# A bf16 three-part spread of 1/den, selectors built ahead of q, two ones columns in kv, and a later slot for one batch's numerators

The chip is one Trainium2, of which one core is used. The metric is the device time of one execution in microseconds (us); a run is repeated and the median quoted. TensorE is called PE here, VectorE DVE, ScalarE ACT and GpSimd POOL, as in the profile.

## The reference

Linear attention with phi(x) = elu(x) + 1 over 8 batches of 8 heads, 576 positions and 64 channels, then a two-layer feed-forward on 4608 tokens:

```python
q_p, k_p = phi(q), phi(k)                       # phi(x) = where(x > 0, x, exp(x) - 1) + 1
kv  = einsum('bhsd,bhse->bhde', k_p, v)
z   = k_p.sum(axis=2)
num = einsum('bhsd,bhde->bhse', q_p, kv)
den = einsum('bhsd,bhd->bhs', q_p, z) + 1e-6
x   = (num / den) -> [4608 tokens, 512]
h   = x @ w_in        # 512 -> 2048
g   = h - tanh(h)
out = g @ w_out       # 2048 -> 512
```

## The kernel before

The tokens go through the feed-forward in nine chunks (c = 0 to 8) of 512. While PE works on chunk c, the attention of batch c + 1 is threaded between its matmuls: lists s1 and s2 name what is emitted after the n-th group of four layer-one matmuls and after the n-th group of four layer-two matmuls (a slot). All loads are issued by POOL and cast to bf16 on the way. The parts that matter here (cuts marked `# ...`):

```python
def a_kv_cols(b, banks):                  # kv and z of batches 2 to 7
    ps = [banks()[:, 0:272].rearrange("p (i e) -> p i e", i=2) for hg in range(2)]
    for i in range(2):
        for j in range(J):                # J = 9
            for hg in range(2):           # the two halves of PE's rows, side by side
                r = slice(64 * hg, 64 * hg + 64)
                nc.tensor.matmul(ps[hg][:, i, :], kp[r, i, j]..., vp[r, i, j, :], ...)
    for hg in range(2):                   # vp: 128 columns of v and 8 columns of ones
        nc.vector.tensor_mul(kz_t[b][:, hg, :, 0:136], ps[hg], mask[:, hg, :, 0:136])

def b0_spread(pairs, n0):                 # batch 0: 1/den to 128 partitions, fp32 matmuls
    for n, p in enumerate(pairs):
        for t in range(4):
            nc.tensor.matmul(ps_all[:, 4 + t, 128 * (n0 + n):...], sel[r, p]..., rden_t[0][r, 0:128], ...)

# the opening, in order of emission
load_q(0); load_k(0); make_identity(nc, ident); load_v(0)
for f0, n in ((0, 256), (256, 256), (512, 512), (1024, 512), (1536, 512)):
    load_wi(f0, n)
load_k(1); load_wo(0); load_wo(1); load_q(1)
for i in (1, 0):
    nc.gpsimd.memset(v_b[i][:, 2], 1.0)
# ...
load_v(1); load_wo(2); load_wo(3)
# ... kv, den and num of batch 0
b0_spread((0, 2), 0)
b0_scale(0, ns0, 0, 0, 4); b0_scale(0, ns0, 0, 4, 8); b0_scale(2, ns0, 1)
b0_num(1, ns0)
# open2(): b0_spread((1, 3), 2); b0_scale(1, ...); b0_scale(3, ...)

# chunk c, batch n1 = c + 1
for p in range(NP + 1):                   # five numerator groups
    s2[(11 if c == 1 else 9) + p].append(lambda p=p: a_num(n1, p))
```

The first layer-one matmuls of chunk 0 are ordered by hand: two groups on pair 0 (halves of 256 columns), then open2, then the rest.

## Time and profile before

| | before |
|---|---|
| median (3 runs) | 294.0 us (293.95 to 294.2) |
| profiled span | 291.8 us at full PE clock |
| PE busy / DVE / ACT | 97% / 60% / 48% |
| transfers, 4 to 50 us | 197 to 209 GB/s without a pause |
| one 128x512 matmul, start to start | 216 ns |

In a profile line such as those in the prediction, the columns are: start (us from the span's start), length, engine, source line, operation, output<-inputs, shapes, count, and in brackets how long the engine sat idle before it and what released it. Lines of the chain of work that ended last have start, length and what it was. A busy PE is modelled, so pace is judged from matmul starts.

### The profile page before, as it was taken

Reading aid. Unit: us, or ns where it says so; the run is one execution under the profiler, and the core shown is the slowest. Engines: PE = TensorE matmul, PEld = TensorE weight load, DVE = VectorE, ACT = ScalarE, POOL = GpSimd, SP = SyncE. Lnnn points to the kernel's source line nnn. Section 1 sums busy time; section 2 is a strip of 40 time slices with the busy share of each in tenths; the row PEclk is TensorE's granted clock in tenths of the full one; section 3 lists DMA queues with packets and bytes.
Section 4 is the critical chain, followed back from the end, with each engine's and each line's share of the span. In section 5 each row is a group of like instructions: output and inputs, shape, how many; then the busy total and the mean of one; then the engine's idle time right before and its main releaser. Section 6 shows DMA issues by size and latency. Waiting matters only on the chain.

```text
span 291.8 us, 4476 instructions
## 1 busy us (share of the span) xinstructions
PE 284.2 (97%) x1775; PEld 134.5 (46%) x1803; DVE 174.8 (60%) x266; ACT 139.7 (48%) x168; POOL 33.1 (11%) x55
## 2 busy tenths in 40 slices
PE   8999999999999999999999999999999999999994
PEld 3544464454454444544444445444444444444443
DVE  4759958987458674776478637865581457106600
ACT  4838638846254733465345534751551155126411
POOL 8673030110030003000300030000000000000000
PEclk9999999999999999999999999999999999999999
DMA  6999999998989668955795579766117310130032
GB/s 96 198 204 212 208 207 213 214 168 145 253 158 159 170 131 135 200 139 127 134 223 131 120 137 196 144 142 139 32 34 168 73 36 0 42 84 20 0 74 72
DMA packets 39077, 38.94 MB, mean 133 GB/s; under 512 B 16336, under 2 KB 33808, under 8 KB 38288
## 3 DMA queue, kind: packets, MB, share of 16 engines
q0 software_dynamic: 17552, 18.35, 39.0%
q1 hardware_dynamic: 21344, 20.17, 30.5%
q8 instruction: 14, 0.23, 0.3%
q10 hardware_dynamic: 160, 0.13, 0.1%
q14 instruction: 7, 0.06, 0.1%
HBM read 43.91 MB, written 9.55 MB: 183 GB/s over the span
## 4 chain that ended last, share of the span: by engine, by line
PE 75%; DMA 18%; POOL 2%; issue 1%; SPq 1%; DVE 1%; ACT 1%; DVEq 0%; POOLq 0%
PE ps_all L366 37%; PE ps_all L387 32%; DMA w_out_sb<-in_moe_w_out_dram 6%; DMA w_in_sb<-in_moe_w_in_dram 3%; DMA rdb<-ds 3%; DMA out_dram<-osb 2%; PE ps_all L199 2%; DMA kraw<-in_k_dram 2%; PE ps_all L317 2%; DMA ds<-rden 1%; PE ps_all L276 1%; POOL v L419 1%; ACT osb L396 1%; SPq L401 0%; POOL qraw L90 0%
## 5 line engine op out<-in xcount | busy, mean ns | idle before, releaser
L366 PE MATMUL ps_all<-xT,w_in_sb 128*128 128x512 bf16 x558 | 126.5, 380 | 0.9 <-issue 0.2
L387 PE MATMUL ps_all<-w_out_sb,gT 128*128 128x512 bf16 x548 | 126.2, 380 | 0.7
L373 DVE TENSOR_TENSOR gT<-ps_all,th 128x1024 bf16<-128x1024 f32 x64 | 77.9, 1218 | 59.7 <-ACT th L372 59.7
L372 ACT ACTIVATE th<-ps_all 128x1024 f32<-128x1024 f32 x64 | 65.5, 1023 | 57.0 <-PE ps_all L366 46.4
L366 PEld LDWEIGHTS <-w_in_sb 128*128 128x128 bf16 x574 | 55.0, 98 | 66.0
L387 PEld LDWEIGHTS <-gT 128*128 128x128 bf16 x560 | 54.1, 98 | 64.7 <-issue 0.6
L396 ACT COPY osb<-ps_all 128x512 f32<-128x512 f32 (+1 forms) x36 | 20.8, 582 | 72.3 <-PE ps_all L387 55.9
L328 DVE TENSOR_TENSOR xT<-ps_all,rdb 128x512 bf16<-128x512 f32 x24 | 16.3, 689 | 13.7 <-PE ps_all L317 11.2
L134 ACT ACTIVATE e<-qraw 128x1152 bf16<-128x1152 bf16 x16 | 18.5, 1161 | 7.3 <-DMA qraw<-in_q_dram 7.3
L134 ACT ACTIVATE e<-kraw 128x1152 bf16<-128x1152 bf16 x15 | 17.4, 1162 | 0.1
L136 DVE TENSOR_TENSOR qp<-e,r 128x1152 bf16<-128x1152 bf16 x16 | 12.1, 758 | 7.8 <-ACT e L134 7.0
L136 DVE TENSOR_TENSOR kp<-e,r 128x1152 bf16<-128x1152 bf16 x15 | 11.4, 758 | 7.9 <-ACT e L134 7.0
L383 POOL COPY g<-qT 1x1 bf16<-1x1 bf16 x5 | 0.9, 182 | 119.7 <-DMA qT<-qp 119.7
L378 DVE TENSOR_TENSOR gT<-ps_all,th 128x512 bf16<-128x512 f32 x16 | 10.3, 686 | 2.3 <-ACT th L377 1.7
L377 ACT ACTIVATE th<-ps_all 128x512 f32<-128x512 f32 x16 | 9.2, 598 | 4.4 <-PE ps_all L366 3.2
L444 PE MATMUL ps_all<-zero 128*128 128x512 bf16 x29 | 9.3, 487 | 1.2 <-DVE zero L405 1.2
L317 PE MATMUL ps_all<-qT,kz 128*128 128x512 bf16 x28 | 10.1, 380 | 0.1
L135 DVE TENSOR_SCALAR r<-qraw 128x1152 bf16<-128x1152 bf16 x16 | 7.3, 453 | 1.9 <-DMA qraw<-in_q_dram 1.9
L199 PEld LDWEIGHTS <-kp 64*128 64x128 bf16 x216 | 6.4, 94 | 2.5 <-issue 2.5
L285 DVE RECIPROCAL rden<-den 128x144 f32<-128x144 f32 x7 | 7.4, 1052 | 0.2
L199 PE MATMUL ps_all<-vp,kp 64*128 64x136 bf16 x216 | 7.4, 220 | 0.0
L394 DVE COPY osb<-ps_all 128x128 f32<-128x128 f32 x1 | 0.3, 291 | 11.6 <-DMA out_dram<-osb 11.6
(84 smaller groups left out, 123.0 us busy)
## 6 DMA issues: line engine op xcount, KB each, us to landing
out_dram<-osb SPq DMA_DIRECT2D x70, 128.0 KB
rdb<-ds SPq DMA_DIRECT2D x12, 576.0 KB
kraw<-in_k_dram POOLq DMA_DIRECT2D x7, 576.0 KB, 7.1
qraw<-in_q_dram POOLq DMA_DIRECT2D x7, 576.0 KB, 9.2
v<-in_v_dram POOLq DMA_DIRECT2D x7, 576.0 KB, 11.9
w_out_sb<-in_moe_w_out_dram POOLq DMA_DIRECT2D x4, 512.0 KB, 16.0
w_in_sb<-in_moe_w_in_dram POOLq DMA_DIRECT2D x6, 256.0 KB, 8.6
qraw<-in_q_dram POOLq DMA_DIRECT2D x2, 288.0 KB, 4.4
```

The source lines that it names most:

```text
L134: return (lambda: nc.scalar.activation(e, x, AF.Exp), lambda: nc.vector.tensor_scalar(r, x, 0.0, 1.0, ALU.max, ALU.add), lambda: nc.vector ...
L136: lambda: nc.vector.tensor_tensor(y, e, r, ALU.min))
L199: nc.tensor.matmul(ps[hg][:, i, :], kp[r, i, j].rearrange("p h d -> p (h d)"), vp[r, i, j, :], start=(j == 0), stop=(j == J - 1))
L317: nc.tensor.matmul(ps, kz[:, p // 2, p % 2, 0:128], qT[:, p % 2, 0:8, p // 2, :], start=True, stop=True)
L328: nc.vector.tensor_mul(xT[:, p, S * b:S * b + 512].rearrange("p (j t c) -> p j t c", j=8, t=4), ps.rearrange("p j (t c) -> p j t c", t=4), ...
L366: nc.tensor.matmul(h, w_in_sb[:, 2 * (p % 2) + p // 2, fi * 128:(fi + 1) * 128], xT[:, p, c * 512:(c + 1) * 512], start=(n == 0), stop=(n ...
L372: nc.scalar.activation(th, h, AF.Tanh)
L373: nc.vector.tensor_sub(gT[:, fi:fi + 2, :], h, th)
L378: nc.vector.tensor_sub(gT[:, fi, :], h, th)
L387: nc.tensor.matmul(o, gT[:, fi, i * 128:(i + 1) * 128], w_out_sb[:, fi, :], start=(fi == 0), stop=(fi == NF - 1))
L396: nc.scalar.copy(osb[:, f0:f1], o[:, f0:f1])
L444: nc.tensor.matmul(ps_all[:, 0, :], zero[:, 0:128], zero, start=True, stop=True)
```

## The change

Its intent: make the second 1/den spread of batch 0 cheap (bf16 matmuls with 1/den split into three bf16 parts, where the trace has two records for each fp32 one), have the selectors ready long before, stream fewer columns in kv, and keep batch 2's numerators from meeting their late broadcast.

```diff
-    vp = const.tile([128, 2, J, 136], BF16, name="vp")
+    vp = const.tile([128, 2, J, 130], BF16, name="vp")
 ...
-        ps = [banks()[:, 0:272].rearrange("p (i e) -> p i e", i=2) for hg in range(2)]
+        ps = [banks()[:, 0:260].rearrange("p (i e) -> p i e", i=2) for hg in range(2)]
 ...
-            nc.vector.tensor_mul(kz_t[b][:, hg, :, 0:136], ps[hg], mask[:, hg, :, 0:136])
+            nc.vector.tensor_mul(kz_t[b][:, hg, :, 0:128], ps[hg][:, :, 0:128], mask[:, hg, :, 0:128])
+            nc.vector.tensor_mul(kz_t[b][:, hg, :, 128:136], ps[hg][:, :, 128:129].to_broadcast([128, 2, 8]),
+                                 mask[:, hg, :, 128:136])
 ...
+    def b0_split():                       # two halves, each a cast and a scalar_tensor_tensor
+        f = rden_t[0][:, 0:128]
+        nc.vector.tensor_copy(t1, f)
+        nc.vector.scalar_tensor_tensor(u, t1, part[:, 0:1], f, ALU.mult, ALU.add)
+        yield
+        nc.vector.tensor_copy(t2, u)
+        nc.vector.scalar_tensor_tensor(w, t2, part[:, 1:2], u, ALU.mult, ALU.add)
+        rden_t[0] = w
+        yield
+    def b0_spread3(pairs, n0):            # as b0_spread, with the bf16 selector sel3 and w
 ...
     load_q(0)
+    make_identity(nc, ident)
     load_k(0)
-    make_identity(nc, ident)
 ...
+    prepare()                             # selectors: moved here, ahead of phi(q), from s2[0] of chunk 0
 ...
     b0_kz(1)
+    next(split0)
     b0_spread((0, 2), 0)
 ...
     b0_scale(2, ns0, 1)
+    next(split0)
     b0_num(1, ns0)
     def open2():
-        b0_spread((1, 3), 2)
+        b0_spread3((1, 3), 2)
 ...
-                s2[(11 if c == 1 else 9) + p].append(lambda p=p: a_num(n1, p))
+                s2[min(12 + p, 15) if c == 1 else 9 + p].append(lambda p=p: a_num(n1, p))
 ...
-            order = [((0, 0), (0, 1)), ((2, 0), (2, 1), (0, 2), (0, 3), (2, 2), (2, 3)),
+            order = [((0, 0), (0, 1)), ((0, 2), (0, 3), (2, 0)), ((2, 1), (2, 2), (2, 3)),
                      [(p, fi) for p in (1, 3) for fi in range(4)]]
-                if n == 1:
+                if n == 2:
                     open2()
```

More of the change, by code (lines that the diff above doesn't have):

```diff
@@ L233, in b0_num @@
         nc.scalar.copy(ns[:, i::2, 0:8, :].rearrange("p a j t -> p a (j t)"), ps_all[:, b0:b0 + 2, :])
+    def b0_split():
+        f = rden_t[0][:, 0:128]
+        t1, t2, w = (rpool.tile([128, J * 16], BF16, name=n)[:, 0:128] for n in ("t1", "t2", "w"))
+        u = rpool.tile([128, J * 16], F32, name="u")[:, 0:128]
+        nc.vector.tensor_copy(t1, f)
[6 more added lines that the diff above has]
+    def b0_spread3(pairs, n0):
+        for n, p in enumerate(pairs):
+            for t in range(4):
+                r = slice(32 * t, 32 * t + 32)
+                nc.tensor.matmul(ps_all[:, 4 + t, 128 * (n0 + n):128 * (n0 + n) + 128],
+                                 sel3[r, p].rearrange("p h e -> p (h e)"), rden_t[0][r], start=True, stop=True)
     def b0_spread(pairs, n0):
@@ L419 @@
         nc.gpsimd.memset(v_b[i][:, 2], 1.0)
-    nc.gpsimd.memset(vp[:, :, :, 128:136], 1.0)
+    nc.gpsimd.memset(vp[:, :, :, 128:130], 1.0)
     load_v(1)
@@ L439, with prepare @@
         rest -= e0
+    def prepare():
+        for t in range(4):
+            nc.vector.tensor_copy(s8[32 * t:32 * t + 32].rearrange("q n h p -> q (n h p)"),
+                                  ident[32 * t:32 * t + 32, 32 * t:32 * t + 24])
+        s24 = rpool.tile([128, 2 * NP], F32, name="s24")
+        f8 = s8.rearrange("q n h p -> q n (h p)")
+        nc.vector.tensor_add(s24, f8[:, 1], f8[:, 2])
+        nc.vector.tensor_reduce(part[:, 0:1], s24, mybir.AxisListType.X, ALU.add, negate=True)
+        nc.vector.tensor_reduce(part[:, 1:2], f8[:, 2], mybir.AxisListType.X, ALU.add, negate=True)
+        nc.vector.tensor_add(s24, s24, f8[:, 0])
+        nc.vector.tensor_copy(
+            sel3, s24.rearrange("q (h p) -> q p h", h=2).unsqueeze(3).to_broadcast([128, NP, 2, 64]))
     def spin(n):
@@ L457 @@
     a_qT_pe(0, 1, side, "AA")
-    for t in range(4):
-        nc.scalar.copy(s8[32 * t:32 * t + 32, 0].rearrange("q h p -> q (h p)"),
-                       ident[32 * t:32 * t + 32, 32 * t:32 * t + 8])
     nc.scalar.copy(sel, s8[:, 0].rearrange("q h p -> q p h").unsqueeze(3).to_broadcast([128, NP, 2, 64]))
@@ L477 @@
     b0_kz(1)
+    split0 = b0_split()
+    next(split0)
     b0_spread((0, 2), 0)
@@ L482 @@
     b0_scale(2, ns0, 1)
+    next(split0)
     b0_num(1, ns0)
     def open2():
-        b0_spread((1, 3), 2)
+        b0_spread3((1, 3), 2)
         b0_scale(1, ns0, 2)
         b0_scale(3, ns0, 3)
-    def prepare():
-        for t in range(4):
-            nc.vector.tensor_copy(s8[32 * t:32 * t + 32, 1:3].rearrange("q n h p -> q (n h p)"),
-                                  ident[32 * t:32 * t + 32, 32 * t + 8:32 * t + 24])
-        s24 = rpool.tile([128, 2 * NP], F32, name="s24")
-        f8 = s8.rearrange("q n h p -> q n (h p)")
-        nc.vector.tensor_add(s24, f8[:, 1], f8[:, 2])
-        nc.vector.tensor_reduce(part[:, 0:1], s24, mybir.AxisListType.X, ALU.add, negate=True)
-        nc.vector.tensor_reduce(part[:, 1:2], f8[:, 2], mybir.AxisListType.X, ALU.add, negate=True)
-        nc.vector.tensor_add(s24, s24, f8[:, 0])
-        nc.vector.tensor_copy(
-            sel3, s24.rearrange("q (h p) -> q p h", h=2).unsqueeze(3).to_broadcast([128, NP, 2, 64]))
     for c in range(NC):
@@ L526 @@
             s2[4].append(lambda: (a_qphi(1, 1), load_q(2), load_k(2), load_v(2)))
-            s2[0].append(prepare)
             s2[7].append(lambda: (a_qT_pe(1, 0, side), a_kv(1, side), a_qT_pe(1, 1, side)))
```

## The prediction

> **What bounds the kernel now.** I read the page's busy table, then the chain of work that ended last, then the timeline of the stretches where TensorE (PE) has a gap. PE is the bound: it is busy 97% of 291.8 us, and the granted clock is 1.00 throughout. Busy is not peak, so I checked the pace: between 233 and 274 us the chain shows runs such as 38 layer-one matmuls in 8.37 us, 220 ns each, hardly above the 216 ns of four in 0.86 us elsewhere. Only work taken off PE, or a gap closed on PE, moves the end.
>
> ```profile
> PE 284.2 (97%) x1775; PEld 134.5 (46%) x1803; DVE 174.8 (60%) x266; ACT 139.7 (48%) x168; POOL 33.1 (11%) x55
> L366 PE MATMUL ps_all<-xT,w_in_sb 128*128 128x512 bf16 x558 | 126.5, 380 | 0.9 <-issue 0.2
> L199 PE MATMUL ps_all<-vp,kp 64*128 64x136 bf16 x216 | 7.4, 220 | 0.0
> ```
>
> The chain, however, does not run back through PE to the start. Asked for the first 60 us alone it reads (start, length, what):
>
> ```profile
> 2.78 6.18 DMA kraw<-in_k_dram
> 9.24 8.93 DMA w_in_sb<-in_moe_w_in_dram
> ...
> 22.39 0.66 POOL v L93
> 23.05 17.84 DMA w_out_sb<-in_moe_w_out_dram
> 40.89 0.04 issue
> 40.93 0.38 PE ps_all L387
> ```
>
> So the third quarter of w_out lands at 40.89 us and the first layer-two matmul that needs it starts 0.04 us later. Everything PE does before 40.9 us is off the path that sets the end, unless it becomes later than that landing. The busy table by stretches says why the landing is where it is: the columns are stretch, total, PE, PEld, DVE, ACT, POOL, clock, DMA share, GB/s.
>
> ```profile
> 4.00:24.00 20.00, 18.95 (x202) 9.88 (x202) 12.65 (x25) 12.94 (x21) 15.26 (x25) 1.00 1.24 197
> 24.00:41.00 17.00, 16.89 (x120) 8.88 (x120) 14.47 (x32) 11.17 (x17) 2.78 (x4) 1.00 1.23 209
> ```
>
> The transfers run at about 200 GB/s without a pause, and w_out's third quarter waits 17.84 us behind others already queued. It is limited by transfer rate, not by when it is issued. And PE already waits for it:
>
> ```profile
> 40.20 0.68 PE L164 MATMUL ps_all<-ident,qp 128*128 128x128 bf16 x9
> 40.93 1.02 PE L387 MATMUL ps_all<-w_out_sb,gT 128*128 128x512 bf16 x3
> ```
>
> The nine transposes' weight loads take 0.51 us from 40.19, so the next matmul could go at about 40.72; it goes at 40.93. PE is some 0.2 us early already.
>
> The opening, which most of the change concerns, is a ladder of short waits (the timeline, PE and DVE):
>
> ```profile
> 14.72 0.42 DVE L225 TENSOR_TENSOR kz<-ps_all,mask 128x256 bf16<-128x256 f32 x1
> 15.64 1.35 DVE L244 TENSOR_TENSOR xT<-ns,ps_all 128x256 bf16<-128x256 f32 x3 [0.50 <-PE ps_all L240]
> 16.09 1.01 ACT L233 COPY ns<-ps_all 128x1024 f32<-128x1024 f32 x1 [0.97 <-DVE xT L244]
> 16.12 0.71 PE L577 MATMUL ps_all<-xT,w_in_sb 128*128 128x256 bf16 x4
> 17.05 0.73 PE L240 MATMUL ps_all<-rden,sel 32*128 32x128 f32 x16 [0.22 <-DVE xT L244]
> ```
>
> The second spread of 1/den (17.05) starts only when DVE's third scaling ends (15.64 + 1.35 = 16.99).
>
> Batch 2's numerators meet a late DMA in the second chunk:
>
> ```profile
> 77.20 0.38 PE L317 MATMUL ps_all<-qT,kz 128*128 128x512 bf16 x1
> 77.41 1.03 PE L387 MATMUL ps_all<-w_out_sb,gT 128*128 128x512 bf16 x4
> 77.80 1.89 DVE L328 TENSOR_TENSOR xT<-ps_all,rdb 128x512 bf16<-128x512 f32 x3 [2.49 <-DMA rdb<-ds]
> 78.54 0.38 PE L317 MATMUL ps_all<-qT,kz 128*128 128x512 bf16 x1
> ```
>
> DVE waits 2.49 us for the broadcast 1/den, and the third numerator waits for its bank: its matmul could go at 77.41 + 4 x 0.216 = 78.27 and goes at 78.54, a gap of 0.27 us on PE.
>
> **What the skill says.** The Trainium skill, "PSUM — Partial Sum Buffer", section "PSUM bank collisions raise a hardware error", wants accesses guarded by bank. The trace agrees: the second spread writes other columns of the four banks that the third scaling reads, and starts 0.06 us after it. "FP8 and Floating Point Precision", "TensorE Precision Notes", gives true fp32 four passes. The trace agrees in direction: eight fp32 spread matmuls take 0.73 us (16 records), eight bf16 ones of batch 1, a little wider, 0.30 us. "TensorE: Matmul & The Clock Gate", section "Wait — 56ns, not 53.3ns?", spaces warm matmuls by columns / 2.4 GHz plus 2.5 ns: 216 ns for 512, as measured. "SBUF — State Buffer", "Who interferes with whom", says that DVE's two-port modes lock GpSimd out while it writes descriptors; no row of this trace shows such a lock by itself.
>
> **The change part by part.**
>
> *Selectors earlier.* The preparation takes 34.06 to 35.81, 1.75 us of DVE, in a stretch where PE streams without a gap: removing it there is worth nothing on PE. Its new place is after the masks (DVE is free at 3.50) and before the first q (5.42): 3.50 + 1.75 = 5.25, so it fits. Even 0.7 us late is harmless, as the next step waits for ACT until 6.6. Four ACT casts (0.81 us) go, but ACT's copy at 14.11 then waits for PE anyway (its matmuls end at 14.07): zero. The identity moved ahead of k delays k's issue by 0.6 us (2.78 to 3.4), but q occupies the transfers until about 6.7, so k's landing should not move.
>
> *Split and spread.* Batch 1's row of split operations took 0.24 + 0.37 us per half (44.78 to 45.43); for 128 columns about 0.22 + 0.35. The first half runs after kz: 15.16 to 15.78, so the first scaling goes from 15.64 to about 15.8 (0.15 later). The third scaling then ends near 17.15, and the second half ends near 17.75: the new spread can go at about 17.85, where the old one went at 17.05. It frees PE at 18.1 (0.23 us until the next matmul in batch 1, 46.16 to 46.39) against 17.93. But three more layer-one matmuls stand before it. The first two of those write banks 2 and 3, which ACT reads until 16.09 + 1.01 = 17.10; so they go at 17.2, and all three end at 17.85. Then three more until 18.75, a wait for the scaled pair (spread ends about 18.15, scaling of 0.68 until 18.9), then eight: 18.95 + 8 x 0.216 = 20.68. Before: 17.93 + 14 x 0.216 = 20.95. Gain 0.27 us, all of it before 40.9 us. It should turn into a longer wait for w_out: 0.2 + 0.27 = about 0.5 us. Value at the end: zero.
>
> *130 columns for 136.* The 36 matmuls of a batch run as 18 pairs on two halves of the rows, 1.17 us a batch in the chain, so 65 ns a pair with the switch of mode, close to the columns' 59 ns by the formula above. Six columns fewer save 6 / 2.4 = 2.5 ns a pair: 18 x 2.5 = 45 ns, six batches 0.27 us, an estimate. DVE pays: two operations become four. The main one stays near 0.42 (256 columns took 424 ns, 272 took 430), and the new one of 16 elements costs about 0.17 (a 128x32 copy took 184 ns), so some 0.3 us more a batch. kz was ready at 60.47 in the second chunk and used at 61.06; at 60.8 it still is in time, and later chunks have a slot more.
>
> *Num of batch 2 a slot later.* It closes the 0.27 us gap, as the broadcast is there by 77.8. But the fourth and fifth numerators now share the last slot. The fourth's matmul goes at about 80.24; DVE, after the third (to 80.27) and a copy of v (0.45, to 80.72), scales it until 81.41. Layer one of the next chunk reaches its fourth matmul at 80.57 + 3 x 0.216 = 81.22 and waits till 81.48. Gap back: 0.26. Net near zero, from -0.27 to +0.1.
>
> Sum: 0 (opening) - 0.27 (columns) + 0 (batch 2) = -0.27, so 294.0 - 0.27 = 293.7; some weight for a part of the gaps staying closed gives **293.6 us**.
>
> **Rivals.** (a) The opening's gain survives: then w_out would have to land earlier. For it: the chain calls the transfer the releaser by semaphores, an inference. Against: 209 GB/s up to that moment and a matmul within 0.04 us. It would give about 293.2. (b) DVE's new work before q starves the descriptors, or the later issue of k opens a hole in the transfers; then w_out lands later, and every us of hole is one of time. For it: transfers dip between 6 and 7 us to 133 GB/s. Against: k's descriptors are there 2 us before q is through. At 0.6 us it gives 294.2. (c) DVE becomes the bound by its 0.3 us a batch: it is at 63% between 81 and 233 us (95.37 of 152), so this would need the den matmuls to wait; about 294.2. (d) The 130-wide rows are read no faster than 136: 293.9.
>
> **Range and chances.** No part can be worth 5.9 us (2%): the whole change touches under 1 us of PE time, and PE's gaps before the tail add up to about 2 us. Range 293.0 to 294.3: low is (a) with batch 2's gap kept closed, high is (b) or (c). Faster 0.01, same 0.98, slower 0.01.
>
> **What would show it.** After: the second spread near 17.85 with bf16 matmuls; the first tanh some 0.2 us earlier; the matmul on w_out still at 40.9 with a longer wait (right) or at 40.6 (rival a); the kv group at about 1.12 us in the chain instead of 1.17; no wait at the third numerator of batch 2, but one at the fourth layer-one matmul after it. The prediction is wrong if w_out lands at another time, or if DVE's extra small operations put den matmuls behind.

## The result

The changed kernel takes 294.03 us (median of 5, 293.63 to 294.69) against 294.1 (5 runs, 293.95 to 294.2). The ratio is 1.000, with a 95% interval of 0.9986 to 1.0015: the same. A ratio here is the mean time of one kernel's fast runs over the mean of the other's in the same rounds, so it isn't quite the ratio of the quoted medians.

The kv group of the page after (PE is busy 98% of the span, 97% before):

```profile
L199 PE MATMUL ps_all<-vp,kp 64*128 64x130 bf16 x216 | 7.3, 217 | 0.0
```

The chain of work that ended last still runs through the third quarter of w_out:

```profile
22.80 18.29 DMA w_out_sb<-in_moe_w_out_dram
41.10 0.04 issue
41.14 1.02 PE ps_all L410 x4
```

It lands at 41.10 instead of 40.89, and the matmul on it goes 0.04 us later, as before. The opening, timeline of the changed kernel:

```profile
15.83 0.71 PE L600 MATMUL ps_all<-xT,w_in_sb 128*128 128x256 bf16 x4
16.62 0.22 DVE L245 CAST t<-u 128x128 bf16<-128x128 f32 x1
16.87 0.81 PE L389 MATMUL ps_all<-xT,w_in_sb 128*128 128x512 bf16 x3 [0.33 <-ACT ns L235]
16.88 0.35 DVE L246 SCALAR_TENSOR_TENSOR w<-t,part,u 128x128 bf16<-128x128 bf16 x1
17.61 0.29 PE L255 MATMUL ps_all<-w,sel 32*128 32x128 bf16 x8
18.02 1.29 DVE L267 TENSOR_TENSOR xT<-ns,ps_all 128x512 bf16<-128x512 f32 x2 [0.79 <-PE ps_all L255]
18.76 3.33 PEld L389 LDWEIGHTS <-w_in_sb 128*128 128x128 bf16 x16 [0.39 <-issue]
```

The spread itself is short as intended (0.29 against 0.73 us), but there are two pauses around it: PE waits for ACT's copy before the three layer-one matmuls (16.87), and for the scaled pair after the next three (18.76).

Batch 2's numerators in chunk 1 and the start of chunk 2:

```profile
77.82 0.69 DVE L351 TENSOR_TENSOR xT<-ps_all,rdb 128x512 bf16<-128x512 f32 x1 [2.33 <-DMA rdb<-ds]
80.41 0.38 PE L340 MATMUL ps_all<-qT,kz 128*128 128x512 bf16 x1
80.83 0.69 DVE L351 TENSOR_TENSOR xT<-ps_all,rdb 128x512 bf16<-128x512 f32 x1
81.57 4.20 PEld L389 LDWEIGHTS <-w_in_sb 128*128 128x128 bf16 x20 [0.30 <-issue]
```

The fourth group is scaled from 80.83 to 81.52, and the layer-one matmul that needs it goes at 81.57. Its three predecessors started at 80.74, 80.96 and 81.17, so it could have gone at 81.39: a gap of 0.18 us on PE, as foretold (0.26 was the figure).

### The profile page after: what moved, and what is told of

It is laid out like the page before. It is cut to its first block, busy times and chain, and to the rows that moved or that the text cites. A ratio compares the mean times of both kernels' runs of the same rounds, so it can differ in the third digit from the quotient of the medians.

```text
span 291.9 us, 4500 instructions
## 1 busy us (share of the span) xinstructions
PE 285.3 (98%) x1795; PEld 133.8 (46%) x1795; DVE 177.6 (61%) x282; ACT 138.9 (48%) x164; POOL 33.0 (11%) x55
## 4 chain that ended last, share of the span: by engine, by line
PE 82%; DMA 13%; POOL 2%; issue 1%; ACT 0%; SPq 0%; DVE 0%; POOLq 0%
PE ps_all L389 38%; PE ps_all L410 38%; DMA w_out_sb<-in_moe_w_out_dram 6%; DMA w_in_sb<-in_moe_w_in_dram 3%; PE ps_all L199 2%; DMA kraw<-in_k_dram 2%; PE ps_all L340 2%; DMA out_dram<-osb 2%; PE ps_all L299 1%; POOL v L442 1%; POOL qraw L90 0%; ACT osb L419 0%; PE ps_all L343 0%; SPq L424 0%; POOL qraw L93 0%
## 5 line engine op out<-in xcount | busy, mean ns | idle before, releaser
L389 PE MATMUL ps_all<-xT,w_in_sb 128*128 128x512 bf16 x574 | 127.9, 379 | 0.5 <-ACT ns L235 0.3
L410 PE MATMUL ps_all<-w_out_sb,gT 128*128 128x512 bf16 x560 | 127.5, 379 | 0.2 <-DMA w_out_sb<-in_moe_w_out_dram 0.2
L134 ACT ACTIVATE e<-kraw 128x1152 bf16<-128x1152 bf16 x15 | 17.4, 1162 | 0.0
L199 PE MATMUL ps_all<-vp,kp 64*128 64x130 bf16 x216 | 7.3, 217 | 0.0
```

Of the source, the lines that this page charges most:

```text
L134: return (lambda: nc.scalar.activation(e, x, AF.Exp), lambda: nc.vector.tensor_scalar(r, x, 0.0, 1.0, ALU.max, ALU.add), lambda: nc.vector ...
L199: nc.tensor.matmul(ps[hg][:, i, :], kp[r, i, j].rearrange("p h d -> p (h d)"), vp[r, i, j, :], start=(j == 0), stop=(j == J - 1))
L389: nc.tensor.matmul(h, w_in_sb[:, 2 * (p % 2) + p // 2, fi * 128:(fi + 1) * 128], xT[:, p, c * 512:(c + 1) * 512], start=(n == 0), stop=(n ...
L410: nc.tensor.matmul(o, gT[:, fi, i * 128:(i + 1) * 128], w_out_sb[:, fi, :], start=(fi == 0), stop=(fi == NF - 1))
```

## The experiments

Three measures recur, all from the starts of matmuls in a run's trace. **The landing** is the start of the first matmul on the third quarter of w_out. **The wait for w_out** is the time from the last transpose before it, less the 0.055 us that this takes when nothing is waited for. **The rest** is the time from the landing to the last matmul. Execution to execution, the landing scatters; the rest repeats to 0.01 us where no transfer plays into it.

| kernel | landing | wait | rest | chunk 1 | chunk 2 |
|---|---|---|---|---|---|
| before | 40.93 | 0.23 | 246.89 | 30.62 | 30.35 |
| changed | 41.14 | 0.40 | 246.72 | 30.34 | 30.52 |
| a1 changed again | 41.71 | 0.41 | 246.71 | 30.34 | 30.52 |
| a2 kv columns alone | 41.27 | 0.40 | 246.54 | 30.34 | 30.34 |
| a3 later slot alone | 41.74 | 0.41 | 246.80 | 30.35 | 30.53 |
| a4 opening alone | 41.14 | 0.09 | 246.94 | 30.67 | 30.36 |
| b1 before, light loads | 40.99 | 0.00 | 246.68 | 30.41 | 30.36 |
| b2 changed, light loads | 44.12 | 0.00 | 246.72 | 30.34 | 30.52 |
| b3 widths | 41.16 | 0.41 | 246.70 | 30.46 | 30.32 |
| b4 changed, fourth group earlier | 41.55 | 0.42 | 246.54 | 30.34 | 30.34 |
| c1 changed, light, memsets late | 40.50 | 0.00 | 246.71 | 30.34 | 30.52 |
| c2 changed, memsets early | 42.09 | 0.00 | 246.72 | 30.34 | 30.52 |
| c3 before, kv and slots mended | 41.15 | 0.42 | 246.36 | 30.31 | 30.31 |
| c4 changed, all mended | 41.09 | 0.47 | 246.36 | 30.31 | 30.31 |

("Chunk 1" is from the start of layer one of chunk 1 to that of chunk 2. In the four runs with wait 0.00 the first matmul on that quarter of w_out goes when PE gets to it.)

### a1: the changed kernel again

No edit.

> The changed kernel once more. Theory (the landing of w_out's third quarter sets the end): the span minus that landing is a constant of the kernel, 250.84 us as in its first trace (291.94 - 41.10; the kernel before had 291.85 - 40.89 = 250.96), while the landing itself scatters by some 0.3 us from execution to execution. Rival (the change itself, by the later issue of k or DVE's work beside it, pushes the landing back by 0.2 us): the landing is again 41.05 to 41.15 and never as early as 40.9. Either way the time should be within 0.2% of before.

Measured: 293.87 us (5 runs), ratio to before 1.0001 (0.9988 to 1.0013). The landing was 41.71, the rest 246.71 against 246.72 the first time. So the landing isn't fixed at 41.05 to 41.15, as the rival had it: over the five profiles with full loads and the old opening it was 40.93 to 41.74 (mean 41.25), over the five with the new opening, in their usual memset order or a later one, 41.09 to 41.71 (mean 41.33). With a scatter of 0.8 us, five profiles each can't exclude a mean shift of 0.2 us, but nothing here asks for one. The kernel before happened to be profiled with the earliest landing of all.

### a2, a3, a4: one part at a time

a2 is the kernel before with the hunk on `vp` and `a_kv_cols`; a3 has only the slot line; a4 has all but these two parts.

> Kernel before with the 130-column kv alone. My step on record: 45 ns a batch, 0.27 us in six. From the first trace of the changed kernel, the block from the last matmul before to the first after it went from 1.483 to 1.468 us, so 15 ns a batch. Theory after the trace: 1.468 us again, span minus landing 250.96 - 0.09 = 250.87. Step on record: 1.438 us and 250.69. Rival (DVE's two more operations cost PE time): the den matmuls of some chunk start later against the chunk's first matmul than before, and span minus landing is 250.96 or more.

> Kernel before with batch 2's numerators a slot later alone. Step on record: the 0.27 us gap at the third numerator goes, a gap of 0.26 us comes at the fourth layer-one matmul of the next chunk; span minus landing 250.96 +0.0/-0.1. Rival (author's intent): no new gap, 250.7.

> Kernel before with the selectors built early and the second spread in three bf16 parts, and nothing else. Theory: the first layer-one tanh comes 0.2 to 0.3 us earlier than in the kernel before (20.29), the wait for w_out grows by as much, span minus landing stays 250.96 within 0.04, time 294.0 to 294.2. Rival (opening's gain reaches the end): time 293.7 or less and the matmul on w_out earlier than 40.75.

Measured, medians of 5: a2 293.75 us (ratio 0.9992, 0.9980 to 1.0005), a3 293.82 (0.9999), a4 293.87 (1.0000), none clear of 1. The traces are sharper.

- **a2:** the kv block, from the last matmul ahead of it to the first one after it, took 1.468 us in the changed kernel against 1.483 before, 15 ns and not 45, and a2's chunks are 30.34 against 30.355 us, the same 15 ns. DVE's two extra operations per batch cost PE nothing: the chunk is shorter by exactly what the kv block is. The rest of 246.54 is 0.35 under that of before; 0.09 are the columns (6 x 0.015), and 0.27 are luck: the broadcast 1/den came early enough in this execution that batch 2 had no gap.
- **a3:** chunk 1 without a gap (30.35), chunk 2 with the new one (30.53, 0.18 more). The old gap depends on when the broadcast 1/den lands: read at the third numerator's matmul, it was 0.27 (before), 0.32 (a4), 0.16 (b3), 0.06 (b1) and 0.00 (a2), and it follows the start of DVE's first scaling, 27.24 us after the start of chunk 1 in a2, 27.60 in the kernel before and 27.65 in a4. The new one was 0.18 in all six traces with the new slots (a3's and five of the changed kernel's). The move exchanges a varying gap of 0.16 us on average for a fixed one of the same size.
- **a4:** the gain of the opening doesn't exist. From the first layer-one matmul to the first on w_out PE takes 14.98 us in the kernel before and 15.02 with the new opening, and the fifth group of layer one starts at 4.62 and 4.66 us after that first matmul. From the first kv matmul of batch 0 to the first layer-one matmul it is 4.22 us in both. My expectation of an earlier first tanh failed (20.63 against 20.29; 0.30 of the difference is v landing later in this execution). PE came so late here that w_out was only 0.09 us behind it, and the chain that ended last runs back through PE to batch 0's v and not through w_out: the two paths are within a few tenths of each other.

Why the prediction had 0.27 us there: it started the second half of the old opening at 17.93, the first matmul record after the spread. The weight-load line of the same stretch of the kernel before shows the loads beginning sooner:

```profile
17.70 1.19 PEld L366 LDWEIGHTS <-w_in_sb 128*128 128x128 bf16 x7
```

The single records have two loads, at 17.703 and 17.717, ahead of the matmul at 17.932: one matmul record, of about 17.715, is missing. The light run of the same opening (b1) has it, 1.59 us after the first layer-one matmul, which is 17.71 here. The old opening was 0.22 us better than I read it. The page shows that records are lost (PE x1775 for PEld x1803); a count (64 layer-one matmul records where this stretch issues 66) would have shown it.

### b1, b2: taking w_out's wait away

To see whether the opening matters once no transfer stands in its way, half a MB of w_in is left out in both kernels (wrong result, relative error 0.74; same instructions on PE):

```diff
+        f = fi if fi < 12 else fi - 4
-        nc.tensor.matmul(h, w_in_sb[:, ..., fi * 128:(fi + 1) * 128], ...)
+        nc.tensor.matmul(h, w_in_sb[:, ..., f * 128:(f + 1) * 128], ...)
-    for f0, n in (..., (1024, 512), (1536, 512)):
+    for f0, n in (..., (1024, 512)):
```

> Kernel before with its last quarter of w_in not loaded (blocks 12 to 15 of the hidden width use the weights of blocks 8 to 11, so the result is wrong on purpose): half a MB less to move, 2.5 us at 207 GB/s, ahead of q, v and w_out's later quarters. Same instructions on PE. Theory: w_out's third quarter lands near 38.5, PE no longer waits for it; the matmul on it goes where PE gets to it, near 40.7, and the span falls by the wait of 0.2 us and no more: 291.65, time 293.85. Rival (PE's wait was something else, or the whole start is paced by transfers): the span falls by 1 us or more.

> The changed kernel with the same quarter of w_in left out (wrong result on purpose). Theory: now the opening's gain is no longer swallowed: the matmul on w_out goes 0.25 to 0.3 us earlier than in the light kernel before, and the span is lower by that plus the 0.12 us after the landing: 0.35 to 0.45 us under it, time near 293.45. Rival (opening's gain lost elsewhere, for instance at batch 1's q or by ACT and DVE pacing the first chunk): not over 0.15 us under it.

b1: 293.37 us against 293.83 of before (5 and 11 runs), ratio 0.9985 (0.9973 to 0.9997), span 291.72. The wait for w_out is gone, and what comes back at the end is about 0.45 us of 294. So transfers do hold the start, by a few tenths (0.1 to 0.8 us by the interval). The theory's 0.2 us was what before's luckiest profile showed; others waited 0.4. The table's wait isn't all of it, which the prediction and the theory both missed: in several profiles PE has already waited for batch 1's v ahead of the last transposes, as in the changed kernel:

```profile
38.63 1.66 PE L177 MATMUL ps_all<-v,kp 64*128 64x192 bf16 x36 [0.22 <-DMA v<-in_v_dram]
```

From the first layer-one matmul to the last of these transposes PE takes 24.53 us in the kernel before and in b1, but 24.61 in a2, 24.74 in a3 and 24.77 in b3 (with the new opening 24.57 in a4, 24.85 in the changed kernel and 25.27 in b4, where batch 1's q is late too). With this the waits of the five profiles with full loads and the old opening average 0.48 us, near the 0.45 that b1 brought.

b2 was a surprise: 296.77 us, 1% slower (0.98%, 0.81 to 1.15%). The timeline of the opening, and the table of the stretch of the pause (stretch, total, PE, PEld, DVE, ACT, POOL, clock, DMA share, GB/s):

```profile
16.85 2.73 DVE L245 CAST t<-u 128x128 bf16<-128x128 f32 x1
17.38 2.10 POOL L443 MEMSET v<- 128x1152 bf16 x2
20.02 0.40 PE L255 MATMUL ps_all<-w,sel 32*128 32x128 bf16 x8 [2.12 <-DVE w L246]
```

```profile
17.06:20.50 3.44, 1.29 (x12) 0.54 (x12) 2.87 (x2) 0.00 (x0) 3.44 (x6) 0.90 1.26 204
```

The cast in the second half of the split, 0.22 us in the changed kernel's profile, took 2.73 us and ended 0.1 us after POOL's memset of v, which the lighter loads had brought forward from 20.0 to 17.4. PE stood still for 2.12 us behind it, and then the granted clock fell to half for 3.41 us (19.84 to 23.25 by the clock's own records). The new opening has put a DVE operation on its critical path that POOL can hold. The Trainium skill has this in "SBUF — State Buffer", section "Who interferes with whom": copies and casts of DVE in two-port modes and POOL instructions take one port pair by turns, the later one blocked to the end of the other. It was cited in the prediction, but not for this cast. The two spans alone don't prove it, hence c1 and c2.

### c1, c2: is it the memset?

c1 is b2 with the memsets issued behind POOL's last load; c2 is the full changed kernel with them moved up behind the second load of k, so that they fall beside the cast:

```diff
 c1:  load_wo(2); load_wo(3)
+     for i in (1, 0): nc.gpsimd.memset(v_b[i][:, 2], 1.0)
 c2:  load_k(1)
+     for i in (1, 0): nc.gpsimd.memset(v_b[i][:, 2], 1.0)
      load_wo(0)
```

> The changed kernel with the last quarter of w_in left out (wrong result on purpose), as in the light run that came out 3 us slower, and with GpSimd's memsets of the ones in v moved behind its last load. In the slower run the cast of the second half of the split took 2.73 us instead of 0.22, beside a memset of v on GpSimd from 17.38 to 19.48. Theory (that memset holds the cast): the cast takes 0.22 again, PE's clock stays at full, time 293.2 to 293.5, and from the start of batch 0's kv to the end it takes 279.35 us (the light kernel before: 279.54, + 0.04 for the opening, - 0.19 after w_out's landing... 0.04 more or less). Rival (the lighter load schedule or the clock is the cause, the memset only coincides): again 2 us or more over 294.

> The changed kernel, all loads, right result, with GpSimd's memsets of v moved up behind the second k's load, so that they run from about 16.4 to 18.6, beside the second half of the split (16.6 to 17.2). Theory (memset holds DVE's cast): the cast ends near 18.6 instead of 16.84, the second spread starts 1.3 us later or more, and the wait for w_out (0.4 us) cannot swallow it: 295 us or more, up to 297 if PE's pause halves its clock. Rival (no such lock): 294.0, the cast 0.22 us.

c1: 293.31 us, ratio 0.9980 (0.9968 to 0.9992). The cast is short again and the clock full (from batch 0's kv to the end it took 279.56 us and not the 279.35 expected, as b1, with hardly a gap at batch 2, had left nothing to gain after the landing):

```profile
16.70 0.22 DVE L245 CAST t<-u 128x128 bf16<-128x128 f32 x1
```

c2: 294.92 us (6 runs, 294.61 to 296.15; I had expected 295 or more), ratio 1.0045 (1.0028 to 1.0062), with a right result:

```profile
16.58 2.07 POOL L439 MEMSET v<- 128x1152 bf16 x2
16.86 1.95 DVE L245 CAST t<-u 128x128 bf16<-128x128 f32 x1
19.25 0.29 PE L255 MATMUL ps_all<-w,sel 32*128 32x128 bf16 x8 [1.34 <-DVE w L246]
```

Adding the overlap makes the cast nine times as long, taking it away restores it: the memset holds the cast. In b2 the cast would have been done by 17.07, before the memset's recorded start at 17.38; spans on POOL are rough, and what held it for those 0.3 us isn't shown. The half clock came in b2's profile, behind the longer pause, and not in c2's, behind 1.34 us. The runs without a trace vary: a mean clock of 0.992 to 0.994 in four of b2's five runs (296.6 to 297.4 us) and 1.000 in the fifth (295.83), and 0.992 and 0.994 in the two slowest of c2's six; so the half clock, as far as these means show it, came more often behind the longer pause, and not only there. "TensorE: Matmul & The Clock Gate", section "What's actually happening", gives half rate after an idle window of about 3.4 us that runs free; the length of 3.41 us agrees, while PE had matmuls within every 3.4 us here.

c1 also bears on the opening: with w_out out of the way in both, 293.31 (c1) and 293.37 (b1) are alike, though timed in other rounds, and PE takes 19.23 and 19.20 us from batch 0's first kv matmul to its first on w_out.

### b3: what a column costs

The kernel before with rows of v and ones 144 wide, another number of streamed columns for each batch, and the change's two DVE operations in place of one (cut here):

```diff
+WIDTHS = {2: 130, 3: 132, 4: 134, 5: 136, 6: 144, 7: 129}
-    vp = const.tile([128, 2, J, 136], BF16, name="vp")
+    vp = const.tile([128, 2, J, 144], BF16, name="vp")
-    nc.tensor.matmul(ps[hg][:, i, :],   ..., vp[r, i, j, :],   ...)
+    nc.tensor.matmul(ps[hg][:, i, 0:w], ..., vp[r, i, j, 0:w], ...)     # w = WIDTHS[b]
```

> Kernel before with rows of v and ones 144 wide (288 bytes), of which batches 2 to 7 stream 130, 132, 134, 136, 144 and 129 columns. Theory A (columns set the pace, but rows of 260 bytes are read more slowly): block from the matmul before to the matmul after, 1.483 us at 136, falls by 7.5 ns a column to 1.438 at 130 and 1.431 at 129, and rises to 1.543 at 144. Theory B (a floor or a rounding in the number of columns, whatever the rows): 130 costs 1.468 here too, and the times are stepped rather than on a line. Only the profile matters.

293.64 us, right result. The chain of work that ended last, batches 2 to 7 in order (start, length):

```profile
58.35 1.13 PE ps_all L201 x36
86.22 1.14 PE ps_all L201 x36
116.55 1.16 PE ps_all L201 x36
146.89 1.17 PE ps_all L201 x36
177.24 1.23 PE ps_all L201 x36
207.66 1.13 PE ps_all L201 x36
```

By matmul starts, the blocks of 130, 132, 134, 136, 144 and 129 columns take 1.438, 1.453, 1.468, 1.483, 1.543 and 1.438 us: a straight line of 7.5 ns a column, as the prediction worked out (129 costs what 130 does). Theory A holds but for its 1.431 at 129 columns. With rows of 130 (260 bytes), the changed kernel takes 1.468, what 134 columns cost: the narrower row gives back two thirds of the gain. What in the reading of the rows costs this is open; only rows of 260, 272 and 288 bytes were run.

### b4, c3, c4: a better version

b4 puts the fourth numerator into slot 14; c3 is the kernel before with 136-wide rows of which 130 columns are streamed, the change's two DVE operations, b4's slots and its old opening; c4 is the changed kernel with both, the memsets late, and the second spread ahead of `(2, 0)`:

```diff
-                s2[min(12 + p, 15) if c == 1 else 9 + p]
+                s2[(12, 13, 14, 14, 15)[p] if c == 1 else 9 + p]        # b4, c3, c4
-    vp = const.tile([128, 2, J, 130], BF16, name="vp")
+    vp = const.tile([128, 2, J, 136], BF16, name="vp")                  # c3, c4, with vp[r, i, j, 0:130]
-            order = [..., ((0, 2), (0, 3), (2, 0)), ((2, 1), (2, 2), (2, 3)),
+            order = [..., ((0, 2), (0, 3)), ((2, 0), (2, 1), (2, 2), (2, 3)),   # c4
```

> The changed kernel with batch 2's fourth numerator in slot 14 beside the third, not in slot 15 beside the fifth. Theory: DVE then has scaled the fourth group by 81.2 and the fourth layer-one matmul of the next chunk needs it at 81.4, so the new gap (0.18 us in the first trace) goes: span minus landing 250.84 - 0.18 = 250.66. Rival (the gap is the bank or the broadcast and moves to the fifth numerator): 250.84.

> Kernel before, its opening untouched, with 130 columns streamed from rows that stay 136 wide (272 bytes) and batch 2's numerators in slots 12, 13, 14, 14, 15. Theory: kv block 1.438 us a batch against 1.483 (0.27 us in six) and no gap at batch 2 (0 to 0.3 us in the runs of before): from the first matmul on w_out's third quarter to the last matmul 246.35 us (before 246.89), time 293.3 to 293.6. Rival (DVE's small operations cost what the columns save): 246.6 or more.

> The changed kernel with 136-wide rows, batch 2's numerators in slots 12, 13, 14, 14, 15, GpSimd's memsets behind its last load, and the second spread one layer-one matmul earlier. Theory: 246.35 us from w_out's third quarter to the last matmul as in the kernel without the new opening; the fifth group of layer one starts 4.35 to 4.45 us after the first layer-one matmul (before 4.62, changed 4.66), all of which goes into the wait for w_out; time as that kernel's within 0.15 us. Rival (opening's gain reaches the end): 0.25 us under it.

b4: 293.74 us (ratio 0.9995, not clear of 1), but the rest is 246.54, 0.18 less than the changed kernel, and chunk 2's gap is gone. Its chain shows the third and fourth numerators together and 24 layer-one matmuls without a break:

```profile
79.91 0.43 PE ps_all L340 x2
80.34 0.86 PE ps_all L410 x4
81.20 0.12 PE ps_all L343 x4
81.32 5.18 PE ps_all L389 x24
```

c3: 293.41 us against 293.68 in the same rounds, ratio 0.9986 (0.9974 to 0.9998); the kv block is 1.438 us for every batch and the rest 246.36, as expected (246.35). c4: 293.46, ratio 0.9989 (0.9976 to 1.0002), rest 246.36. The earlier spread brought nothing here: the fifth group starts at 4.64 us, not at 4.4. The spread went 1.77 us after the first layer-one matmul (1.78 in the changed kernel), because it waited for w, and w was late because the cast took 0.53 us and not 0.22:

```profile
16.70 0.53 DVE L245 CAST t<-u 128x128 bf16<-128x128 f32 x1
17.67 0.29 PE L255 MATMUL ps_all<-w,sel 32*128 32x128 bf16 x8 [0.35 <-DVE w L246]
```

No memset was near. The cast ended 0.03 us after POOL's issue of a load of w_out (16.43 to 17.20), and in a4, where it took 0.52 us, 0.06 us after such an issue; in the four other profiles without a memset beside it, it took 0.22 us beside load issues too. What decides isn't shown, and what the earlier spread is worth stays open (an estimate from these lines: with a cast of 0.22 us it could have gone 0.3 us sooner). The best kernel found is c3, without the new opening: 0.14% under before. It beats the changed kernel too by the rest (246.36 against 246.72), though the two weren't timed in the same rounds.

## Why the prediction was right or wrong

The range and the outcome (same) held; 293.6 was 0.4 us low. Step by step:

- **The bound: right.** w_out's landing sets the end. The matmul on it follows within 0.04 us in both profiles, and taking half a MB of loads away removes the wait and about 0.45 us (b1). Two things qualify it: PE waits for batch 1's v too, and in a4 PE itself was nearly the later. Rival (a), that the opening's gain reaches the end, was never put to the test, since there was no gain. Of rival (b), that the landing moves with the change, the 0.6 us that it needs for 294.2 isn't there: the landings overlap over ten profiles, with means 0.08 us apart.
- **"Gain 0.27 us" in the opening: wrong, though it didn't count.** PE is 0.04 us later. The mis-sized term is the start of the old second half, "17.93 + 14 x 0.216", which is really 17.71: a lost matmul record. That is 0.22 of the 0.31 between 0.27 and -0.04; the rest is the last eight, which start 2.93 us after the first layer-one matmul and not 2.83 (18.95 less 16.12). Two of the signs that were to show the gain came all the same, by luck: the first tanh was 0.25 us earlier (20.04), as v had landed so that kv began 0.29 us earlier (11.61 against 11.90), and the wait for w_out grew to 0.40, as w_out landed later.
- **Split: half right.** The first half took 0.22 and 0.35 as said, but fitted its pause: from batch 0's kv to layer one it's 4.22 us in both kernels, not 0.15 more.
- **Selectors earlier: right in effect.** They ended at about 5.7 instead of 5.25 (the casts took 0.88 and 0.71 us beside POOL's load issues, where before they had taken 0.69, with fewer columns, and 0.43), within the slack of 0.7 us.
- **"Six batches 0.27 us" for the columns: the size failed.** 0.09 us was measured. The rate per column was right (b3), but the rows were narrowed along with it, which gave back 30 ns of 45 a batch. Rival (d) named this; I gave it no weight in the sum.
- **Batch 2 a slot later: right.** The gap of 0.27 went, one of 0.18 came (0.26 predicted). What I didn't see is that the old gap varies from 0 to 0.32.
- **DVE's 0.3 us a batch: right, free.** The operations took 416 and 166 ns, and chunk time fell by exactly the kv block's gain (a2). Rival (c) is refuted.

From landing to last matmul the change is worth 246.89 - 246.72 = 0.17 us in these two profiles, and its landing was 0.21 us later, within the scatter: sum +0.04, the unchanged time. The forecast of "same" was a safe one: the interval of the ratio is 0.15% either way, some 0.4 us, so the timed runs can hardly tell the 0.4 us forecast from nothing. The traces can.

## What to carry to other kernels

Find the point from which the chain runs through the bound engine alone. Work saved ahead of a rate-limited transfer should only lengthen the wait for it (argued here, not shown: no run saved any), and comparing from that landing onward makes hundredths of a microsecond visible where totals scatter by tenths. When a matmul's columns are cut, cut the streamed slice first and leave the row's width alone until it has been measured. Before a DVE cast or copy goes onto a critical path, look at what POOL may be doing beside it: here a memset of 2 us, harmless so far, could stop PE and halve its clock.

## What the Trainium skill lacked or had wrong

- No page gives a figure for the cost of row width for a matmul's moving operand ("SBUF — State Buffer", "Operand start alignment", speaks of legality only; its "Specifications (TRN2)" names 16-byte lines and a penalty for each crossing, and rows of 272 and 288 bytes are whole numbers of such lines, 260 isn't, but no run tested this as the reason): the same 130 columns cost a kv block of 1.438 us from rows of 272 or 288 bytes and 1.468 from rows of 260; 129 columns cost as much as 130.
- "TensorEngine Tiling (Array Packing)", "Key Properties", says that a change of tiling mode drains PE, without a figure: the first matmul on half rows starts 0.311 us after the last full one, where full ones follow at 0.216, so 0.095 us more.
- "TensorE: Matmul & The Clock Gate" ties half rate to an idle window of about 3.4 us: here PE fell to half clock for 3.41 us behind a pause of 2.12 us within a stretch where it was busy 1.29 of 3.44 us.
